# Group 0 of a convolution and mixture kernel: the filter's last product in blocks of 16 frequencies, its first block inside step 1

## The chip, the cores and the metric

The kernel runs on one core of a Trainium2 chip. The metric is the time of one execution on the device in microseconds (us): the median of the runs, 891.58 us before the change, with runs from 891.2 to 893.62. The core has engines that run side by side, each its own instructions in order: TensorE (PE in the profile, with its weight loads as PEld), VectorE (DVE), ScalarE (ACT), GpSimd (POOL) and SyncE (SP), whose queue issues nearly all DMAs here. They wait for each other through semaphores. SBUF is the on-chip memory, PSUM the eight banks into which TensorE writes its products.

## The reference

All data are float32. The convolution part, cut to what matters:

```
x, v: (4, 11456, 128)      pos_emb: (11456, 64)      w1: (64, 64)      w2: (64, 128)
h  = relu(pos_emb @ w1) @ w2 * exp(-0.01 * pos)
u  = x * v
y  = irfft(rfft(u, 2S) * rfft(h, 2S))[:S]      # a long convolution along the sequence
x' = x * y
```

A soft mixture of 8 experts follows on x' (logits, two softmaxes, two small products per expert, and the sum back to 45824 tokens). The change does not touch it.

## The kernel before

**Tiling.** The transform of length 111 x 197 is done as matrix products with tables. The real input leaves J = 99 frequencies k of the short transform to be handled. The 128 channels are taken in G = 8 groups of 16; a group is 64 signals (4 batches x 16 channels), handled as 16 units u of four signals in step 1 and step 3.

**The stages.** First the filter: its hidden layer, and then two products, `filter_first` and `filter_second`, which leave for every frequency a block of F, the spectrum still in terms of the 64 hidden features. Its last product with `w2` (`filter_last`) turns F into the spectrum of all 128 channels. Then for each group: step 1 (`p1`: `first` makes eight pairs of products per unit and `first_out` copies them from PSUM to the tile T), step 2 (`p2`, for four frequencies at a time: products of T with the table W into PSUM, a multiplication by the filter's spectrum on VectorE into a tile `m`, L344, and the two sums that put the complex result back into T, L350 and L351, on GpSimd), step 3 (`p3`, products with `tab3`, copied to E by ScalarE), step 4 and the gate. Step 3 of a group runs together with step 1 of the next. At the end comes the mixture.

**Around the change: group 0.** Group 0's step 1 runs alone. In its step 2 the filter's last product is made on the way: before every eight frequencies, two calls of `filter_last` (four frequencies each) make the spectrum, ScalarE copies it into `ring`, which has two places of eight frequencies, and a DMA writes the part of groups 1 to 7 to the DRAM tensor `hs`. Group 0 takes its own part from `ring`. A place of the ring is written again only when the multiplications that read it are done and its DMA has landed. Between the multiplications VectorE also prepares inputs of group 1's step 1 (`p1_sd`: a product L268, two sums L270, two sums L274; below called a fold), after the 2nd, 6th, 10th and 14th `p2`.

**What sets the order.** Nearly all instructions are wrapped in `inorder`, so each engine runs them as the Python program issues them. PSUM comes from two pools of four banks: `psa` (units 2, 3, 6, 7, ... of step 1 in group 0, and all of step 2, one bank per `p2`) and `psb` (units 0, 1, 4, 5, ... of group 0, and `filter_last`, two banks per call). A bank is used again when its copy or multiplication has read it. The tile `m` has three buffers. The inputs of units 0 to 7 of group 0 lie in the memory of `ring` until step 1 has read them.

Of the kernel before, what the change touches and what calls it, by code (L numbers as in the profile page):

```python
# [13 lines left out]
AF = mybir.ActivationFunctionType  # L14
# [7 lines left out]
J = 99  # L22
# [41 lines left out]
def conv_part(ctx, tc, cp, moe, xf, vf, xi, xe, pos, w1, w2, win, t1x, t1h, wt, t3, t4, hs, scr):  # L64
    nc = tc.nc
# [18 lines left out]
    inorder = tc.keep_in_program_order  # L84
# [11 lines left out]
    HK = 8  # L96
# [112 lines left out]
                                 start=True, stop=True, tile_position=(0, FO * h))  # L209
        nc.scalar.activation(F[:, k0 : k0 + n, :], ps[:, :n, :], AF.Copy)  # L210

    def filter_last(k):

        n = min(4, J - k)
        ps = [psb.tile([N1, 4, G, CG], F32, tag="psb", name=f"fl{s}_{k}") for s in range(2)]
        for i in range(n):
            for s in range(2):
                inorder(nc.tensor.matmul(ps[s][:, i].rearrange("p g c -> p (g c)"),  # L218
                                         lhsT=F[FO * s : FO * s + FO, k + i, :],
                                         rhs=w2s[FO * s : FO * s + FO],  # L220
                                         start=True, stop=True, tile_position=(FO * s, 0)))
        for s in range(2):
            dst = ring[:N1, k // HK % 2, :, k % HK : k % HK + n, CG * s : CG * s + CG]
            inorder(nc.scalar.activation(dst, ps[s][:, :n].rearrange("p k g c -> p g k c"), AF.Copy))  # L224
        if k % HK or k + 4 >= J:
            k0 = k // HK * HK
            n = min(HK, J - k0)
            nc.sync.dma_start(out=hs[:, :, k0 : k0 + n, :].rearrange("g p k x -> p g (k x)"),
                              in_=ring[:HP, k0 // HK % 2, 1:, :n].rearrange("p g k x -> p g (k x)"))
# [100 lines left out]
    def p1(g, u, sd, large=False):  # L330
        first_out(g, u, first(g, u, sd, large))
# [144 lines left out]
    for g in range(G + 1):  # L476

        if g == 0:
            for u in range(NU):
                p1(g, u, sds.pop(u))  # L480
                if u in (9, 11):
                    p1_x(1, PRE + 2 + (u - 9) // 2)
        elif g < G:
            if not pso:
                first_ps.close()
                pso.append(conv_ps.enter_context(tc.tile_pool(name="pso", bufs=2, space=bass.MemoryType.PSUM)))
            def third(us, larges):
                for u, large in zip(us, larges):
                    p3(g - 1, u, large)
                    if u + 2 < NU and u + 2 not in sds:  # L490
                        sds[u + 2] = p1_sd(g, u + 2, nc.vector)

            def behind(u):
                w = u + 6
                if w < NU:
                    p1_x(g, w)
                elif w < NU + PRE and g + 1 < G:
                    p1_x(g + 1, w - NU)

            def spectrum(i0, i1):  # L500
                for k in range(11 * i0, 11 * i1, 11):
                    inorder(nc.sync.dma_start(out=Hs[:HP, k : k + 11], in_=hs[g - 1, :, k : k + 11]))

            large = g > 1
            ps = [first(g, u, sds[u], not large) for u in range(2)]
            third(range(2), (large, large))
            for u in range(2):
                first_out(g, u, ps[u])
                behind(u)
            for w in range(PRE + HV, NU):  # L510
                p1_v(g, w)
            third(range(2, 4), (large, large))
            for u in range(2, 4):
                p1(g, u, sds[u], not large)
                behind(u)
            for b in range(1, NU // 4):
                if b > 1:
                    spectrum(4 * b - 8, 5 * b - 6)
                us = range(4 * b, 4 * b + 4)
                third(us, (large, large, not large, not large))  # L520
                for u in us:
                    p1(g, u, sds[u], large == (u % 4 < 2))
                    behind(u)
            if g + 1 < G:
                for w in range(PRE):
                    p1_v(g + 1, w)
        else:
            x0, x1, x2 = [sm.tile([128, PW], F32, tag="m", name=f"xl_{i}", bufs=3) for i in range(3)]
            spare = [x0, x1, x2] + [spare[i % 2] for i in (next(turns), next(turns))] + [x0, x2]
            turns = count()  # L530
            xvs = [p4_load(g - 1, rb) for rb in ORDER[:5]]
            moe.weights()
            conv_ps.close()
            moe.logit_banks()
            pso[0] = ctx.enter_context(tc.tile_pool(name="psl", bufs=3, space=bass.MemoryType.PSUM,
                                                    reuse_waits="tile"))
            for u in range(NU):
                p3(g - 1, u)
            moe.places()
            moe.steps = _moe(moe)  # L540
            next(moe.steps)

        sds = {}
        nxt_g = g + 1 if g + 1 < G else None

        def ahead(step):
            if nxt_g is None:
                return
            if step == 1:
                for u in range(PRE):  # L550
                    sds[u] = p1_sd(nxt_g, u, nc.vector)
            else:
                for u in range(PRE, PRE + 4):
                    p1_x(nxt_g, u)

        if 0 < g:
            ahead(1)
        ks = list(range(0, J, KB)) if g < G else []
        if g == 0:
            sds = next_sds  # L560
            for i, k in enumerate(ks):
                if k % HK == 0:
                    for w in range(k, min(J, k + HK), 4):
                        filter_last(w)
                p2(g, k)
                if i in (1, 5, 9, 13):
                    u = PRE + i // 4
                    sds[u] = p1_sd(1, u, nc.vector)
            continue
        ex = exs[g % 2]  # L570
        inorder(nc.sync.dma_start(out=ex, in_=xe[g - 1]))
        if g < G:
            xvs = {0: p4_load(g - 1, 0), APART: p4_halves(g - 1, APART), 2: p4_load(g - 1, 2)}
            vcs, done = {}, 0
            for what, n in STEPS:
                if what == "p2":
                    for _ in range(n):
                        p2(g, ks[done])
                        done += 1
                elif what != "gate":  # L580
                    pv = p4(g - 1, n, what)
                    if what:
                        vcs[n] = p4_copy(g - 1, n, pv)
                else:
                    if n == APART:
                        p4_gate_apart(n, xvs[n], pvs[n], vcs[n], ex)
                    else:
                        p4_gate(g - 1, n, xvs[n], pvs[n], vcs[n], ex)
                    if g < G - 1 and n == 5:
                        for u in range(PRE, PRE + HV):  # L590
                            p1_v(g + 1, u)
                    p4_out(g - 1, n, xvs[n])
                    if n == 0:
                        ahead(2)
                    if n in NEXT:
                        xvs[NEXT[n]] = p4_load(g - 1, NEXT[n])
                    if n == 2:
                        xvs[6] = p4_halves(g - 1, 6)
            assert done == len(ks)
            p4_rest(g - 1, ex)  # L600
            continue
        def last_gate(t, rb, xv, pv, vc):
            if t < 4:
                p4_gate(g - 1, rb, xv, pv, vc, ex)
            else:
                p4_gate_apart(rb, [xv[:, PW // 2 * w :][:, : PW // 2] for w in range(2)], pv, vc, ex)
            p4_out(g - 1, rb, xv)
            if t == 5:
                p4_rest(g - 1, ex)
            if t == 3:  # L610
                xvs.append(p4_load(g - 1, ORDER[6]))
            moe.ahead(t)
            if t == 1:
                xvs.append(p4_load(g - 1, ORDER[5]))

        for t, rb in enumerate(ORDER):
            p4(g - 1, rb, 0)
            if t == 6:
                next(moe.steps)
                last_gate(*held)  # L620
            pv = p4(g - 1, rb, 1)
            vc = p4_copy(g - 1, rb, pv)
            held = (t, rb, xvs.pop(0), pv, vc)
            if t == 4:
                moe.spot = wide[rb][:, 0, 2 * NJ : 2 * NJ + 8]
            if t >= 5:
                next(moe.steps)
            if t != 5:
                last_gate(*held)
# [659 lines left out]
```

## Time and profile before

| what | value |
|---|---|
| median of 3 runs | 891.58 us (891.2 to 893.62) |
| profiled execution, span (its own time is given as this alone) | 888.8 us |
| TensorE busy | 858.3 us, 97% |
| VectorE busy | 714.9 us, 80% |
| ScalarE busy | 455.9 us, 51% |
| GpSimd busy | 393.3 us, 44% |
| mean granted TensorE clock | 0.991 |

Busy time of TensorE is that of pipelined instructions whose ends are modelled. Times in the rows are counted from the span's start. In a row of the timeline several like instructions that follow each other stand as one, with their number; what is in square brackets is the time that the engine stood idle before, and who ended it; "issue" there is a wait that the profile can't name. A float32 product of the program appears as two products in the trace.

### The profile page before, as it was taken

The page shows a single profiled execution, that of the slowest core. Times are in us where ns is not written, and L with a number is a line of the kernel's source. Part 1 is how long each engine was busy: PE and PEld are TensorE (multiplying, and loading weights), DVE is VectorE, ACT ScalarE, POOL GpSimd, SP SyncE. Part 2 cuts the span into 40 slices and gives each one's busy share as a digit, 9 for nine tenths or more (in the row PEclk, how much of TensorE's full clock was granted, in tenths as well). Part 3 has the DMA queues.
Part 4 walks back from the last instruction along what each step waited for, and adds up shares of the span by engine and source line. Part 5 has one row for each costly group of instructions (what it writes and reads, how often), then busy time and mean ns, then how long its engine had stood idle before and what let it go on. Part 6 is the DMA issues. An engine that isn't in the chain of part 4 may idle for free. (4 is left out here: it accounts for less than half of the span.)

```text
span 888.8 us, 37282 instructions
## 1 busy us (share of the span) xinstructions
PE 858.3 (97%) x16192; PEld 792.5 (89%) x16192; DVE 714.9 (80%) x1239; ACT 455.9 (51%) x971; POOL 393.3 (44%) x538
## 2 busy tenths in 40 slices
PE   9999999999999999999999999999999999999991
PEld 9998989999999999999999999999999997666540
DVE  5967976898899889988988998899779148886791
ACT  5775558315811751473167128414821637887761
POOL 5003860492088029405910960393079013785750
PEclk9999999999999999999999999999999999999996
DMA  9963685548647755775386476557715979993698
GB/s 329 396 193 117 205 249 148 157 147 269 203 125 210 234 165 141 227 235 167 110 282 201 123 224 207 167 167 238 224 57 166 264 182 374 412 369 121 278 417 364
DMA packets 94386, 197.01 MB, mean 222 GB/s; under 512 B 14330, under 2 KB 55708, under 8 KB 90383
## 3 DMA queue, kind: packets, MB, share of 16 engines
q1 hardware_dynamic: 94046, 194.50, 66.8%
q8 instruction: 127, 2.08, 0.9%
q14 instruction: 37, 0.30, 0.1%
q10 hardware_dynamic: 144, 0.07, 0.0%
q0 software_dynamic: 32, 0.07, 0.0%
HBM read 137.73 MB, written 56.86 MB: 219 GB/s over the span
## 5 line engine op out<-in xcount | busy, mean ns | idle before, releaser
L350 POOL TENSOR_TENSOR T<-m 111x256 f32<-111x256 f32 (+1 forms) x199 | 150.8, 758 | 344.5 <-DVE m L344 344.5
L344 DVE TENSOR_TENSOR m<-p,T 111x1024 f32<-111x1024 f32 (+1 forms) x175 | 200.4, 1206 | 14.4 <-PE p L340 7.0
L360 PE MATMUL p<-tab,T 111*99 111x112 f32 x2048 | 205.4, 260 | 1.5 <-POOL T L351 0.3
L360 PEld LDWEIGHTS p<-tab,T 111*99 111x99 f32 x2048 | 198.8, 170 | 6.5 <-issue 1.6
L340 PE MATMUL p<-T,W 128*64 128x128 f32 (+1 forms) x3168 | 196.7, 276 | 0.4 <-issue 0.3
L420 ACT ACTIVATE vc<-p 128x416 f32<-128x416 f32 x112 | 51.9, 516 | 266.2 <-PE p L411 226.6
L340 PEld LDWEIGHTS p<-T,W 128*64 128x64 f32 (+1 forms) x3168 | 181.8, 127 | 2.7 <-issue 0.9
L411 PE MATMUL p<-tab,E 99*64 99x104 f32 x3584 | 174.1, 252 | 1.1 <-DVE E L373 0.6
L411 PEld LDWEIGHTS p<-tab,E 99*64 99x64 f32 x3584 | 166.4, 136 | 3.1 <-ACT vc L420 0.8
L375 ACT ACTIVATE E<-p 99x448 f32<-99x448 f32 x254 | 132.2, 577 | 63.7 <-PE p L360 57.5
L351 POOL TENSOR_TENSOR T<-m 111x256 f32<-111x256 f32 (+1 forms) x199 | 147.4, 740 | 0.0
L186 ACT ACTIVATE T<-p 128x396 f32<-128x396 f32 x240 | 100.4, 539 | 11.5 <-PE p L174 11.4
L174 PE MATMUL p<-tab1x,x 53*64 53x99 f32 x3648 | 86.7, 246 | 0.2 <-ACT E L224 0.2
L174 PEld LDWEIGHTS p<-tab1x,x 53*64 53x64 f32 x3648 | 79.8, 132 | 4.4 <-ACT E L224 0.4
L436 DVE TENSOR_TENSOR p<-p,vc 128x832 f32<-128x832 f32 x46 | 47.3, 1028 | 10.3 <-ACT vc L420 10.3
L268 DVE TENSOR_TENSOR x<-x,T 128x448 f32<-128x448 f32 x51 | 31.6, 619 | 22.2 <-PE p L174 11.2
L274 DVE TENSOR_TENSOR x<-T 128x224 f32<-128x224 f32 x102 | 39.2, 426 | 1.8
L270 DVE TENSOR_TENSOR T<-x 128x224 f32<-128x224 f32 x102 | 39.2, 425 | 1.7
L224 ACT ACTIVATE E<-fl 111x512 f32<-111x512 f32 (+1 forms) x50 | 26.9, 629 | 21.3 <-PE fl L218 21.3
L444 DVE TENSOR_TENSOR E<-p,E 128x824 f32<-128x824 f32 x36 | 36.6, 1017 | 1.2
L713 ACT ACTIVATE xreg<-pt 128x512 f32<-128x512 f32 (+1 forms) x68 | 35.0, 612 | 0.8 <-PE pt L707 0.7
L344 DVE TENSOR_TENSOR m<-p,E 111x1024 f32<-111x1024 f32 (+1 forms) x25 | 28.7, 1202 | 5.1 <-PE p L340 4.9
(156 smaller groups left out, 972.8 us busy)
## 6 DMA issues: line engine op xcount, KB each, us to landing
x<-in_xf_dram SPq DMA_DIRECT2D x114, 256.0 KB, 4.2
out_dram<-xreg SPq DMA_DIRECT2D x16, 1024.0 KB, 10.5
E<-in_xi_dram SPq DMA_DIRECT2D x37, 412.0 KB, 4.0
T<-in_vf_dram SPq DMA_DIRECT2D x65, 224.0 KB, 5.0
scr<-E SPq DMA_DIRECT2D x67, 206.0 KB, 3.7
T<-hs SPq DMA_DIRECT2D x63, 154.0 KB, 4.5
hs<-E SPq DMA_DIRECT2D x12, 784.0 KB, 4.6
mv<-in_vf_dram SPq DMA_DIRECT2D x42, 224.0 KB, 5.2
```

Of the source, the lines that this page charges most:

```text
L174: inorder(nc.tensor.matmul(ps[h][RP * d : RP * d + RP, i, s, :], lhsT=sd[js, i, s, d, :], rhs=tab1x[js, J * (s + d) : J * (s + d + 1)], st ...
L186: inorder(nc.scalar.activation(dst, src, AF.Copy))
L270: inorder(eng.tensor_tensor(out=vt[:, :, m : m + 2], in0=xr[:, :, 0:2], in1=xr[:, :, 2:4], op=op))
L340: inorder(nc.tensor.matmul(ps[ns, i].rearrange("p b c -> p (b c)"), lhsT=W[:, k0 + i, ns], rhs=Tf[:, :, k0 + i, :], start=True, stop=True, ...
L344: inorder(nc.vector.tensor_mul(m[:, :n].rearrange("p k s e c i -> p k s (e c i)").rearrange("p k s (b c) -> p k s b c", c=CG), ps[:, :n].u ...
L350: inorder(eng.tensor_tensor(out=Ty[:, 0], in0=m[:, :n, 0, 0], in1=m[:, :n, 1, 1], op=ALU.subtract))
L351: inorder(eng.tensor_tensor(out=Ty[:, 1], in0=m[:, :n, 1, 0], in1=m[:, :n, 0, 1], op=ALU.add))
L360: inorder(nc.tensor.matmul(pk[:, i, 2 * s : 2 * s + 2, :].rearrange("p q r -> p (q r)"), lhsT=T[0:N1, s, 2 * k + i, u // 2, :, u % 2], rhs ...
L375: inorder(nc.scalar.activation(dst, src, AF.Copy))
L411: inorder(nc.tensor.matmul(pv[RP * h : RP * h + RP, 2 * k + i, w, :], lhsT=E[:J, r, 2 - 2 * w + s, :], rhs=tab4[:, s, o : o + NJ], start=( ...
L420: inorder(nc.scalar.activation(vc[:, w], pv[:, :, 0, :], AF.Copy, scale=2.0 * w - 1.0))
L436: inorder(nc.vector.tensor_tensor(out=pw, in0=pw[:, 1:2].to_broadcast([128, 2, 4, NJ]), in1=vc, op=ALU.add))
```

## The change

The function `filter_run` makes the last product for up to 16 frequencies in a row (2 x HK), in four calls of `filter_last`. The run of frequencies 0 to 15 stands after unit 7 of group 0's step 1; the others, from 16 on, before every 16 frequencies of step 2. In the third call of each run the copy of the second half (`s` = 1) goes to VectorE in place of ScalarE. Group 1's folds come after the 4th, 8th, 12th and 16th `p2`. What is computed stays the same.

```
     def filter_run(k0):
         for k in range(k0, min(J, k0 + 2 * HK), 4):
             filter_last(k, k == k0 + HK)

@@ filter_last(k, shared)
         for s in range(2):
             dst = ring[:N1, k // HK % 2, :, k % HK : k % HK + n, CG * s : CG * s + CG]
-            inorder(nc.scalar.activation(dst, ps[s][:, :n].rearrange("p k g c -> p g k c"), AF.Copy))
+            src = ps[s][:, :n].rearrange("p k g c -> p g k c")
+            if s and shared:
+                inorder(nc.vector.tensor_copy(out=dst, in_=src))
+            else:
+                inorder(nc.scalar.activation(dst, src, AF.Copy))
@@ step 1 of group 0
             for u in range(NU):
                 p1(g, u, sds.pop(u))
+                if u == NU // 2 - 1:
+                    filter_run(0)
@@ step 2 of group 0
             for i, k in enumerate(ks):
-                if k % HK == 0:
-                    for w in range(k, min(J, k + HK), 4):
-                        filter_last(w)
+                if k and k % (2 * HK) == 0:
+                    filter_run(k)
                 p2(g, k)
-                if i in (1, 5, 9, 13):
+                if i in (3, 7, 11, 15):
                     u = PRE + i // 4
                     sds[u] = p1_sd(1, u, nc.vector)
```

On ScalarE around the second half of step 1, before. In a name such as p_0_8_0 stand the group, the unit and the half; fl_4 is a bank of the filter's last product from frequency 4 on.

```order
L186 ACTIVATE T<-p_0_7_0_986 128x2x198
L186 ACTIVATE T<-p_0_8_0_1006 128x2x198
L186 ACTIVATE T<-p_0_9_0_1026 128x2x198
L186 ACTIVATE T<-p_0_10_0_1048 128x2x198
L186 ACTIVATE T<-p_0_11_0_1068 128x2x198
L186 ACTIVATE T<-p_0_12_0_1090 128x2x198
L186 ACTIVATE T<-p_0_13_0_1110 128x2x198
L186 ACTIVATE T<-p_0_14_0_1130 128x2x198
L186 ACTIVATE T<-p_0_15_0_1150 128x2x198
L224 ACTIVATE E<-fl_0_1170 111x8x4x16
L224 ACTIVATE E<-fl_0_1171 111x8x4x16
```

The same place on ScalarE in the changed program:

```order
L186 ACTIVATE T<-p_0_7_0_986 128x2x198
L232 ACTIVATE E<-fl_0_1006 111x8x4x16
L232 ACTIVATE E<-fl_0_1007 111x8x4x16
L232 ACTIVATE E<-fl_4_1018 111x8x4x16
L232 ACTIVATE E<-fl_4_1019 111x8x4x16
L232 ACTIVATE E<-fl_8_1031 111x8x4x16
L232 ACTIVATE E<-fl_12_1043 111x8x4x16
L232 ACTIVATE E<-fl_12_1044 111x8x4x16
L186 ACTIVATE T<-p_0_8_0_1056 128x2x198
L186 ACTIVATE T<-p_0_9_0_1076 128x2x198
```

Seven copies of the filter stand between the units 7 and 8; the eighth, the second half of fl_8, is VectorE's.

On VectorE at the beginning of step 2, before. m_8 is the multiplication for frequencies 8 to 11, the instructions on x_2 are the fold of unit 2 of group 1.

```order
L188 COPY T<-p_0_15_1_1151 128x2x198
L344 TENSOR_TENSOR m_0_1204<-p_0_0_1195,E 111x1024
L344 TENSOR_TENSOR m_4_1217<-p_0_4_1208,E 111x1024
L268 TENSOR_TENSOR x_2_577<-x_2_577,T 128x8x56
L270 TENSOR_TENSOR T<-x_2_577 128x2x112 x2
L274 TENSOR_TENSOR x_2_577<-T 128x4x56 x2
L344 TENSOR_TENSOR m_8_1260<-p_0_8_1251,E 111x1024
L344 TENSOR_TENSOR m_12_1273<-p_0_12_1264,E 111x1024
L344 TENSOR_TENSOR m_16_1311<-p_0_16_1302,E 111x1024
L344 TENSOR_TENSOR m_20_1324<-p_0_20_1315,E 111x1024
L268 TENSOR_TENSOR x_3_579<-x_3_579,T 128x8x56
```

The same place on VectorE in the changed program:

```order
L188 COPY T<-p_0_15_1_1201 128x2x198
L352 TENSOR_TENSOR m_0_1229<-p_0_0_1220,E 111x1024
L352 TENSOR_TENSOR m_4_1242<-p_0_4_1233,E 111x1024
L352 TENSOR_TENSOR m_8_1255<-p_0_8_1246,E 111x1024
L352 TENSOR_TENSOR m_12_1268<-p_0_12_1259,E 111x1024
L276 TENSOR_TENSOR x_2_577<-x_2_577,T 128x8x56
L278 TENSOR_TENSOR T<-x_2_577 128x2x112 x2
L282 TENSOR_TENSOR x_2_577<-T 128x4x56 x2
L230 COPY E<-fl_24_1303 111x8x4x16
L352 TENSOR_TENSOR m_16_1336<-p_0_16_1327,E 111x1024
L352 TENSOR_TENSOR m_20_1349<-p_0_20_1340,E 111x1024
```

The fold stands two multiplications later, and behind it VectorE's copy of the filter (fl_24), ahead of the next multiplication.

## Rows read from the trace of the kernel before

**Rows 1.** The page: busy us (share of the span), instructions; a queue's packets, MB.

```profile
PE 858.3 (97%) x16192; PEld 792.5 (89%) x16192; DVE 714.9 (80%) x1239; ACT 455.9 (51%) x971; POOL 393.3 (44%) x538
...
q8 instruction: 127, 2.08, 0.9%
```

**Rows 2.** Stretches: length, busy of PE, PEld, DVE, ACT, POOL, clock, DMA, GB/s.

```profile
77.40:126.10 48.70, 48.29 (x826) 44.07 (x824) 44.50 (x47) 26.10 (x49) 39.47 (x48) 1.00 0.69 204
126.10:888.00 761.90, 736.44 (x14036) 676.75 (x14036) 616.95 (x1066) 379.34 (x819) 342.62 (x474) 0.99 0.67 218
```

**Rows 3.** Timeline of VectorE, step 2: start, length, line, operation, number [idle before].

```profile
78.63 2.36 DVE L344 TENSOR_TENSOR m<-p,E 111x1024 f32<-111x1024 f32 x2 [2.46 <-PE p L340]
...
84.80 4.60 DVE L344 TENSOR_TENSOR m<-p,E 111x1024 f32<-111x1024 f32 x4
...
89.97 1.65 DVE L270 TENSOR_TENSOR T<-x 128x224 f32<-128x224 f32 x2
...
93.23 4.60 DVE L344 TENSOR_TENSOR m<-p,E 111x1024 f32<-111x1024 f32 x4
...
110.07 6.87 DVE L344 TENSOR_TENSOR m<-p,E 111x1024 f32<-111x1024 f32 x6
117.81 2.36 DVE L344 TENSOR_TENSOR m<-p,E 111x1024 f32<-111x1024 f32 x2 [0.88 <-PE p L340]
121.72 2.36 DVE L344 TENSOR_TENSOR m<-p,E 111x1024 f32<-111x1024 f32 x2 [1.55 <-PE p L340]
124.30 0.96 DVE L344 TENSOR_TENSOR m<-p,E 111x768 f32<-111x768 f32 x1 [0.23 <-ACT E L224]
...
125.97 0.35 DVE L351 TENSOR_TENSOR T<-m 111x192 f32<-111x192 f32 x1
```

**Rows 4.** Timeline of all engines, the first blocks of eight frequencies.

```profile
75.45 2.00 PE L218 MATMUL fl<-E 64*111 64x128 f32 x32
...
76.61 2.16 ACT L224 ACTIVATE E<-fl 111x512 f32<-111x512 f32 x4 [0.57 <-PE fl L218]
...
77.39 2.04 PE L340 MATMUL p<-T,W 128*64 128x128 f32 x32
...
79.35 1.80 PEld L218 LDWEIGHTS fl<-E 64*111 64x111 f32 x32 [0.18 <-issue]
...
80.51 2.17 ACT L224 ACTIVATE E<-fl 111x512 f32<-111x512 f32 x4 [1.74 <-PE fl L218]
```

**Rows 5.** Timeline of all engines, the beginning of step 3.

```profile
126.15 3.41 PE L360 MATMUL p<-tab,T 111*99 111x112 f32 x32 [0.29 <-POOL T L351]
...
129.18 1.89 ACT L375 ACTIVATE E<-p 99x448 f32<-99x448 f32 x4 [4.99 <-DMA hs<-E]
...
129.78 3.31 PE L360 MATMUL p<-tab,T 111*99 111x112 f32 x32 [0.22 <-ACT E L375]
...
130.43 0.69 DVE L270 TENSOR_TENSOR T<-x 128x224 f32<-128x224 f32 x2
```

**Rows 6.** Timeline of VectorE, the last units of step 1.

```profile
74.92 1.26 DVE L188 COPY T<-p 128x396 f32<-128x396 f32 x2 [1.60 <-PE p L174]
```

**Rows 7.** Groups by line from 20 to 140 us: count, busy us, mean ns, idle before.

```profile
L188 DVE COPY T<-p 128x396 f32<-128x396 f32 x16 | 9.1, 571 | 9.8 <-PE p L174 8.5
```

**Rows 8.** Timeline of TensorE's products, step 1.

```profile
66.23 1.50 PE L174 MATMUL p<-tab1x,E 53*64 53x99 f32 x58 [0.29 <-issue]
67.50 0.24 PE L174 MATMUL p<-tab1x,x 53*64 53x99 f32 x1
...
69.68 2.97 PE L174 MATMUL p<-tab1x,mv 53*64 53x99 f32 x127 [0.47 <-issue]
73.92 1.60 PE L174 MATMUL p<-tab1x,mv 53*64 53x99 f32 x63 [1.27 <-issue]
```

**Rows 9.** The page's groups: count, busy us, mean ns of one, idle before.

```profile
L224 ACT ACTIVATE E<-fl 111x512 f32<-111x512 f32 (+1 forms) x50 | 26.9, 629 | 21.3 <-PE fl L218 21.3
```

**Rows 10.** Timeline of GpSimd in step 2.

```profile
111.36 0.74 POOL L350 TENSOR_TENSOR T<-m 111x256 f32<-111x256 f32 x1 [1.46 <-DVE m L344]
112.05 0.74 POOL L351 TENSOR_TENSOR T<-m 111x256 f32<-111x256 f32 x1
```

More of the change, by code (lines that the diff above doesn't have):

```diff
@@ L210, in filter_second, with filter_run, filter_last @@
         nc.scalar.activation(F[:, k0 : k0 + n, :], ps[:, :n, :], AF.Copy)
-    def filter_last(k):
+    def filter_run(k0):
+        for k in range(k0, min(J, k0 + 2 * HK), 4):
+            filter_last(k, k == k0 + HK)
+    def filter_last(k, shared):
         n = min(4, J - k)
```

## The prediction, written before the changed kernel ran

> **What bounds the kernel now.** I read the page's busy shares first. TensorE is busy 97% of the span, VectorE 80% [rows 1], and everything that the change touches lies in group 0, so the share of the whole says little and the stage has to be read by itself. The table by stretches does that: from the first product of group 0's step 2 (77.4) to the first of the next step (126.1) TensorE is busy 48.3 of 48.7 us, but VectorE also 44.5 and GpSimd 39.5; after it TensorE is busy 736 of 762 us [rows 2]. So a shift at 126 us should pass on to the end nearly whole, and inside the stage two engines are close to the bound. VectorE's timeline shows how close: from 84.80 to 116.94 its instructions follow each other without a wait, in cycles of 8.43 us for 16 frequencies (84.80 to 93.23: four multiplications L344 in 4.60, then the five instructions of a fold `p1_sd`). It is behind TensorE there. Only after the last fold does it catch up and wait (0.88 and 1.55 us) [rows 3]. TensorE's own 16 frequencies take 7.8 us (75.45 to 79.35 for eight) [rows 4]. In step 2, then, TensorE never waits because VectorE's arrears, 0.6 us a cycle, just fit into four product banks. Step 3 begins at 126.15, when VectorE's L351 (125.97 plus 0.35) and GpSimd are through; its third unit begins at 129.78, when the copy that waited for the last `hs` write is done [rows 3, 5].
>
> Step 1 of group 0 is the other place. A unit takes 0.69 us there (two VectorE copies end 1.26 us after the first began, a copy is 0.57 long) [rows 6, 7]. But TensorE pauses "for issue" at 66.23, 69.68 and 73.92, each time after 128 products, 3.45 and 4.24 us apart, where 128 products need 2.76 [rows 8]. Instruction fetches are a queue of their own [rows 1], so I read these pauses as TensorE running ahead of them.
>
> **The change part by part.** The sum is made against the profiled execution, span 888.8 us. The median of the runs shown is 891.58; I take the 2.8 us between them as work outside the span that does not change.
>
> *The first 16 frequencies amid step 1.* Removed at the end of step 1: the block of eight at 75.45, 1.94 us [rows 4]. Added after unit 7: four calls of `filter_last`, begun where unit 8 began, at 67.50 [rows 8]. Each call takes two of four banks of `psb`, so the third and fourth call need the copies of the first and second. A block's first copy starts 1.16 us after its first product (75.45 to 76.61), four copies take 2.16 and one is 0.63 long, so they start 0.51 apart [rows 4, 9]. The third call's second bank is free 1.16 + 0.51 + 0.63 = 2.30 us after the run's start, the fourth's 1.16 + 3 x 0.51 + 0.63 = 3.32; that call is half of a block's 1.80 [rows 4], and the run ends at 4.2. It would be 3.6 without the two waits. Unit 9 needs the bank of the fourth call's second copy: 4.2 + 0.29 + 0.51 + 0.63 = 5.6 (0.29 is 1.16 less the first call's 0.87 to 0.9). Units 9 to 15 take 7 x 0.69, so the last ends at 67.50 + 5.6 + 4.8 = 77.9. Now a cover is gone: step 2's first product waits for unit 15's copies, which ended 0.88 us after its last product (unit 15 began at 73.92 + 0.69, its copy ended at 74.92 + 1.26) [rows 6, 8], and were hidden by the block at 75.45. That makes 78.8 against 77.39, with the pauses at 69.68 and 73.92 (0.7 and 1.5 us beyond 2.76) already taken as gone, since the run gives the fetch 4 us. They come back in part: the next 128 products begin at 71.7, unit 12 is due 3.5 us later, step 2 another 3.6 us on, and the fetch has needed 3.45 to 4.24: 0 to 0.8 and 0 to 0.6 us. I take 0.7 for both. Term A: **+2.1 us** (1.4 to 2.8).
>
> The Trainium skill, "Runtime: NRT & Kernel Launch", Instruction fetch mechanics, says that instructions come in blocks of 256 and that the fetch is mostly hidden. The trace agrees on the block (128 products, each with its weight load) and not on the hiding. Were the pauses not fetches, they would stay; that is the fourth rival.
>
> *Step 2 in blocks of 16.* Per 16 frequencies one change from the filter's products to the main ones and one back go away. Eight frequencies take 3.90 us (75.45 to 79.35), of which the products themselves need about 3.6 (1.80 a block by the weight loads), so 0.3 a pair [rows 4]. Against it stand the waits of the second half of a run for banks, 0.6 as above. TensorE alone would gain 1.8 (two more of the calls that left step 2, at 0.9) + 6 x 0.3 and lose 5 x 0.6: about -0.5 us.
>
> *VectorE's copies.* One in each full run, five of them in step 2. The trace has no such copy; a copy of 396 columns takes 0.57 [rows 7], a multiplication of 1024 columns 1.2 and 1.13 to the next (6.87 for six) [rows 3], so 512 columns take between 0.5 and 0.7; by the slope between the two, 0.69 long and 0.61 to the next. It stands behind a fold and ahead of the multiplications of its own frequencies, so everything queued behind it moves by 0.61: a cycle becomes 9.04. The folds move from i = 1, 5, 9, 13 to 3, 7, 11, 15, behind four multiplications as before, so GpSimd has the same arrears beside them and I keep 8.43. (Alone, a pair of a fold's instructions takes 0.69 instead of 1.65 [rows 3, 5].)
>
> VectorE from step 2's first product T: 1.24 until the first multiplication (77.39 to 78.63) [rows 3, 4], four cycles 36.2, so T + 37.4. The run of frequency 80 needs the bank that the copy of 72 then leaves: 4.2 of run, 0.1 of change, 1.24 to the first multiplication of 80: T + 42.95, where VectorE is free at 37.4 + 4 x 1.13 + 0.61 = 42.55. Four more, 4.53, and the tail from 124.30 to 126.32, 2.02 [rows 3]: T + 49.5. GpSimd works off the last eight at 2 x 0.69 [rows 10], from T + 38.6 to T + 49.7. Step 3 starts at about T + 49.6; before it was 126.15 - 77.39 = 48.76. Term B: **+0.85** (0, if the folds shorten and TensorE bounds, to 1.7, with copies of 0.7 and waits at each turn of banks).
>
> *The rest.* ScalarE loses six copies, but it stood idle 1.74 us ahead of a block [rows 4]; nothing. The loads of x_4 and x_5 go behind two `hs` writes on the SP queue, more than 20 us ahead of their folds; nothing. The last `hs` write moves with the run of 96 and lands no later relative to step 3 than now.
>
> Sum: 2.1 + 0.85 = +2.95 us, 891.58 + 3 = **894.6 us**.
>
> **The rivals.** (1) TensorE bounds step 2, because the folds fall where GpSimd is idle: 16 half-fold instructions at 0.35 instead of 0.83 give VectorE 7.7 us back. For it: VectorE waited at the end of the stage. Against: GpSimd is 39.5 of 48.7 us busy. Then B is -0.5 and the time 891.58 + 2.1 - 0.5 = 893.2. (2) Faster: the filter's first run lies wholly in TensorE's pauses. It decides whether ScalarE empties banks as fast as TensorE fills them, so that a run takes 3.6 and not 4.2, in step 1 and five times in step 2, and unit 9 does not wait; with no pause returning, A is 2.1 - 0.6 - 0.6 - 0.7 = 0.2 and B -0.5 - 5 x 0.6 = -3.5: 888.3. Against: two copies need 1.02 us to start, a call 0.9, and VectorE would have to shed the same 3 us. (3) The delay arises but is absorbed behind 129.78, where TensorE has 25 us of idle time to the end [rows 2]: 891.6. Against: its third unit now waits only 0.22 for a landing [rows 5]. (4) The pauses belong to units 6, 10 and 14, not to fetches, and stay: 2.2 - 0.7 = 1.5 more, 896.1. Against: the even 128 products.
>
> **How the numbers follow.** Forecast 0.57, (1) 0.19, (2) 0.08, (3) 0.09, (4) 0.07. The forecast's own range, from its terms' bounds, is 893.0 to 896.1. The whole range, 891.8 to 896.6, leaves out (2) and ends of the others. A measurement of this kernel tells about 0.3% from no change, 2.7 us: 888.9 to 894.25. Of the forecast three quarters lie above (the hand-overs between the engines are not in the sum, and each adds), of (4) nearly all: 0.43 + 0.07 = 0.50 slower; of (1) and (3) nearly all lie inside, with a quarter of the forecast: 0.42; faster 0.08.
>
> **What would show it.** In step 1 of the new profile: the main products of step 2 starting at about 79.5, VectorE's first multiplication 1.2 later, TensorE waiting for ScalarE twice in the run after unit 7, no long issue pause at units 10 and 14. In step 2: VectorE without waits in cycles of 9.0 us until the last fold, TensorE waiting for VectorE's copies before the runs of 64 and 80, step 3 at 129. The forecast is wrong if VectorE waits for TensorE between folds (then 1), if the runs have no inner wait (2), or if step 3 starts late and the end does not (3).

## The result, and the profile after

The changed kernel takes **897.16 us** (median of 5 runs, 893.2 to 900.24) beside 891.25 for the kernel before in the same session: ratio 1.0059, 95% interval 1.0036 to 1.0082, or +5.3 us (3.2 to 7.3). It is slower. The forecast was +2.95 us, so its direction held and its sum was 2.3 us short; the median lies 0.6 us above the upper end of the whole range (896.6).

The profiled execution was the shortest of the five, 893.2 us with a span of 891.2. Its page hardly differs from [rows 1]; the stretches that answer to [rows 2] follow, with the columns given there:

```profile
78.90:128.70 49.80, 48.74 (x792) 44.36 (x793) 47.59 (x52) 20.38 (x37) 39.38 (x48) 1.00 0.57 170
128.70:890.20 761.50, 736.28 (x14036) 676.73 (x14036) 616.78 (x1066) 378.93 (x819) 342.65 (x475) 0.99 0.67 218
```

Behind step 3's first product nothing has changed: 762.5 us to the span's end (891.2 - 128.7), before 762.6. The loss lies ahead of 128.7. TensorE's products in step 1, which answer to [rows 8], and VectorE's timeline of step 2, which answers to [rows 3]:

```profile
60.80 5.73 PE L174 MATMUL p<-tab1x,E 53*64 53x99 f32 x256
66.46 4.49 PE L222 MATMUL fl<-E 64*111 64x128 f32 x64
70.88 1.92 PE L174 MATMUL p<-tab1x,x 53*64 53x99 f32 x62
...
78.89 3.88 PE L348 MATMUL p<-T,W 128*64 128x128 f32 x64 [1.86 <-issue]
...
128.70 0.41 PE L368 MATMUL p<-tab,T 111*99 111x112 f32 x2 [0.49 <-POOL T L358]
```

```profile
72.92 4.70 DVE L188 COPY T<-p 128x396 f32<-128x396 f32 x7 [0.46 <-PE p L174]
80.13 4.62 DVE L352 TENSOR_TENSOR m<-p,E 111x1024 f32<-111x1024 f32 x4 [2.50 <-PE p L348]
...
88.56 0.68 DVE L230 COPY E<-fl 111x512 f32<-111x512 f32 x1
89.16 4.60 DVE L352 TENSOR_TENSOR m<-p,E 111x1024 f32<-111x1024 f32 x4
...
98.18 4.60 DVE L352 TENSOR_TENSOR m<-p,E 111x1024 f32<-111x1024 f32 x4
...
121.08 0.69 DVE L230 COPY E<-fl 111x512 f32<-111x512 f32 x1 [0.25 <-PE fl L222]
122.19 5.48 DVE L352 TENSOR_TENSOR m<-p,E 111x1024 f32<-111x1024 f32 x5 [0.42 <-PE p L348]
```

In the kernel before, step 1 began here:

```profile
61.44 4.49 PE L174 MATMUL p<-tab1x,E 53*64 53x99 f32 x194
```

Step 2 starts 18.09 us behind step 1 (78.89 - 60.80; before 77.39 - 61.44 = 15.95), step 3 another 49.81 later (128.70 - 78.89; before 48.76). The three pauses of [rows 8] have become one, ahead of step 2: unit 15's last copy ended at 77.62 (72.92 + 4.70) and the first main product came 1.27 us after. VectorE runs without a wait from 80.13 to 120.8, in cycles of 9.02 to 9.03 us (80.13, 89.16, 98.18). This execution, the fastest, fits the forecast (+2.14 for a term of 2.1, +1.05 for 0.85). In the first term that is in part luck: the pause beyond the copies was 0.57 us longer than the 0.7 that I took, but the pause at 66.23 [rows 8], which I had left in, was gone, and the run with its copies took 0.14 less. The median doesn't fit, so something that varies from execution to execution is missing.

### The profile page after: what moved, and what is told of

Read it like the earlier page. It is cut to its first block, busy times and chain, and to the rows that moved or that the text cites. A ratio compares the mean times of both kernels' runs of the same rounds, so it can differ in the third digit from the quotient of the medians.

```text
span 891.2 us, 37283 instructions
## 1 busy us (share of the span) xinstructions
PE 860.2 (97%) x16192; PEld 794.3 (89%) x16192; DVE 718.5 (81%) x1245; ACT 452.6 (51%) x965; POOL 393.2 (44%) x538
## 5 line engine op out<-in xcount | busy, mean ns | idle before, releaser
L232 ACT ACTIVATE E<-fl 111x512 f32<-111x512 f32 (+1 forms) x44 | 24.3, 624 | 29.7 <-PE fl L222 29.1
L1130 PE MATMUL pw<-cs,so 32*128 32x512 f32 (+2 forms) x192 | 31.8, 610 | 0.7 <-DVE xreg L1137 0.7
```

The source lines that it names most:

```text
L1130: inorder(nc.tensor.matmul(po[:, :na].rearrange("p k t -> p (k t)"), lhsT=so[NSLOT * a : NSLOT * a + NSLOT], rhs=ct[NSLOT * a : NSLOT * a ...
```

## Experiments

Each kernel was compared with runs of the kernel before on its own chip, whose medians were 891.2 to 891.8 us. Packet times below were read from the trace's records of the instruction queue.

**The changed kernel again.** Nothing edited.

> The changed kernel as it is, once more. The sum of the prediction gives +3 us over the kernel before, and the one profiled execution agrees (step 3 begins 2.9 us later, counted from the start of step 1). The five timed runs lie 2 to 9 us higher, with granted clocks of 0.988 to 0.991. Theory 1 (only the sum): a new profile shows the same step 1 and 2 and the median is 894 to 895. Theory 2 (something more, in most executions: the clock falls after the pause between the steps, or the first loads land later): the median is again near 897, and a profile of such an execution has a stretch at clock 0.5 before 130 us, or step 1 begins later than 61.4.

897.0 us; 1.0064 (1.0041 to 1.0088). Its profiled execution, 897.74 us, is a typical one. VectorE and TensorE around the start of step 2, and the stretches behind it:

```profile
73.53 4.71 DVE L188 COPY T<-p 128x396 f32<-128x396 f32 x7 [0.47 <-PE p L174]
83.15 1.23 DVE L352 TENSOR_TENSOR m<-p,E 111x1024 f32<-111x1024 f32 x1 [4.91 <-PE p L348]
...
92.68 4.60 DVE L352 TENSOR_TENSOR m<-p,E 111x1024 f32<-111x1024 f32 x4
```

```profile
61.15 5.99 PE L174 MATMUL p<-tab1x,E 53*64 53x99 f32 x256
...
81.06 5.43 PE L348 MATMUL p<-T,W 128*64 128x128 f32 x64 [3.43 <-issue]
86.41 4.49 PE L222 MATMUL fl<-E 64*111 64x128 f32 x64
...
132.21 0.41 PE L368 MATMUL p<-tab,T 111*99 111x112 f32 x2 [0.44 <-POOL T L358]
```

```profile
81.00:84.40 3.40, 3.34 (x32) 3.34 (x34) 1.23 (x1) 0.00 (x0) 0.00 (x0) 0.51 0.02 5
84.40:88.00 3.60, 3.60 (x64) 3.42 (x62) 3.22 (x3) 0.43 (x1) 3.34 (x5) 0.99 0.00 0
```

The copies were through at 78.24, and the pause lasted 2.82 us beyond them. Then TensorE's granted clock was 0.5 (1.2 GHz) for 3.4 us, and the block of 64 took 5.43 us where it takes 3.88 at 2.4 GHz. From step 1 to step 2 went 19.91 us, from step 2 to step 3 51.15. VectorE's second four multiplications begin 11.62 us behind step 2's start (92.68 - 81.06), where the first profile has 10.27 (89.16 - 78.89): of the 1.55 us of the slower block 1.35 reach the stage. Less these it takes 49.80, term B as in the first profile. The spans of the two executions are 4.1 us apart (895.3 and 891.2), and 3.2 of them lie here: 1.82 ahead of step 2, of which the pause is 1.55 (2.82 less 1.27), and 1.34 in it, by the clock.

**Parts taken back.** `no_step1` puts the first run of 16 back to the head of step 2, `no_vector` gives all copies to ScalarE, `no_folds` takes the four folds out of step 2.

```
no_step1: -                if u == NU // 2 - 1:
          -                    filter_run(0)
          ...
          -                if k and k % (2 * HK) == 0:
          +                if k % (2 * HK) == 0:
no_vector: `if s and shared` made never true
no_folds: -                if i in (3, 7, 11, 15):   (and the fold under it)
```

> The changed kernel with its first run of 16 frequencies at the head of step 2 instead of amid step 1; all else stays. If the run amid step 1 is what costs (the bank waits of unit 9, the bared copies of unit 15), the time falls by about 2 us against the changed kernel. If it only moves work that has to be done somewhere, and the run of 16 waits for its banks wherever it stands, the time stays within 0.5 us of the changed kernel (+3 us over before), TensorE waits for ScalarE at the head of step 2, and the pauses for issue in step 1 are back at units 10 and 14. If the extra time of most executions comes from the pause of TensorE before step 2, it is gone here.

> The changed kernel with all copies of the filter on ScalarE. If VectorE bounds step 2, a cycle of 16 frequencies falls from 9.0 to 8.4 us, step 3 begins about 1 us earlier than in the changed kernel and the time is 1 us lower (+2 us over before). If the banks bound, the fourth call of a run waits for one copy of ScalarE more and the time stays or rises by 0.5 us.

> The changed kernel without the four folds in step 2; they are made in step 3 of group 1, as the other folds of that group. If VectorE bounds step 2, its 16 us of folds no longer count, VectorE waits for TensorE in each block, and the time falls to where TensorE and the banks bound: about 1.2 us below the changed kernel (+2 us over before). If VectorE did not bound, nothing changes (+3). If the cost lies in VectorE alone, the time falls to that of the kernel before or below.

`no_step1`: 894.59 us, 1.0036 (1.0022 to 1.0051), some 2.4 us below the changed kernel (the intervals overlap) although it has the same blocks and copies. TensorE pauses in step 1 again (0.48, 0.98), but not ahead of step 2:

```profile
62.30 6.04 PE L174 MATMUL p<-tab1x,E 53*64 53x99 f32 x253
...
74.24 1.60 PE L174 MATMUL p<-tab1x,mv 53*64 53x99 f32 x63 [0.98 <-issue]
75.78 4.49 PE L222 MATMUL fl<-E 64*111 64x128 f32 x64
80.19 3.88 PE L348 MATMUL p<-T,W 128*64 128x128 f32 x64
```

Its step 2 starts 17.89 us behind step 1 (80.19 - 62.30), hardly earlier than the 18.09 of the changed kernel's fastest execution. By these profiles a first run of 16 in one piece delays step 2 by some 2 us, amid step 1 as at the head of step 2, and what is gone here is the long pause that other executions of the changed kernel have.

`no_vector`: 896.25 us, 1.0052 (1.0034 to 1.007). Step 3 came 49.00 us behind step 2 (128.63 - 79.63), 0.81 less than with the copies (49.81), and VectorE's cycle is 8.43 again (80.88 to 89.31). So the copies make most of term B (0.81 of the 1.05 measured). In the total the interval can't tell it. This profile is of its fastest execution (894.33): step 2 waits for copies and not for issue.

```profile
80.88 4.62 DVE L352 TENSOR_TENSOR m<-p,E 111x1024 f32<-111x1024 f32 x4 [1.99 <-PE p L348]
...
89.31 4.60 DVE L352 TENSOR_TENSOR m<-p,E 111x1024 f32<-111x1024 f32 x4
```

```profile
79.63 3.88 PE L348 MATMUL p<-T,W 128*64 128x128 f32 x64 [1.39 <-DVE T L188]
...
128.63 0.41 PE L368 MATMUL p<-tab,T 111*99 111x112 f32 x2 [0.54 <-POOL T L358]
```

`no_folds`: 896.98 us, 1.0061 (1.0039 to 1.0082): no gain that the intervals show. VectorE now waits for TensorE in every cycle, here twice in one cycle:

```profile
107.50 0.69 DVE L230 COPY E<-fl 111x512 f32<-111x512 f32 x1 [1.43 <-PE fl L222]
109.69 4.62 DVE L352 TENSOR_TENSOR m<-p,E 111x1024 f32<-111x1024 f32 x4 [1.50 <-PE p L348]
```

and a cycle still takes 8.2 us (the next block's multiplications begin at 117.92): TensorE's own bound in blocks of 16. Its pause ahead of step 2 was 3.51 us, again with 3.4 us at a clock of 0.5 behind it.

**A cover over the pause, and the pause moved.** `cover` parts the first run: calls 0 and 4 behind unit 7, 8 and 12 behind unit 15. `shift` puts 44 more products into TensorE's stream, long before step 1.

```
cover: -                if u == NU // 2 - 1:
       -                    filter_run(0)
       +                if u in (NU // 2 - 1, NU - 1):
       +                    for w in (0, 4) if u < NU - 1 else (HK, HK + 4):
       +                        filter_last(w, w == HK)
shift: ...
       -    idle_products(4)
       +    small_products(48)
```

> The first sixteen frequencies' calls are parted: 0 and 4 amid step 1 as in the changed kernel, 8 and 12 behind unit 15, between step 1 and step 2. Theory (bare fetch and clock): the changed kernel loses beyond the forecast because TensorE's pause ahead of step 2, 1.3 to 3.5 us, lies bare, and because a pause of 3.4 us is followed by 3.4 us at a granted clock of 0.5; two calls (2.2 us) put over that place leave a pause under 1.3 us there, no stretch at 0.5, step 2 17.0 to 17.9 us behind step 1, and 893.5 to 894.8 us in all. Rival (the blocks of sixteen cost more in step 2 than forecast, whatever stands ahead of it): 896 to 898 us, as the changed kernel.

> The changed kernel with its four idle products ahead of the filter's first product replaced by 48 small ones (16 columns by 16), so that every later TensorE instruction stands 44 products, or 88 records, later in the stream; nothing else moves. The pauses of step 1 stood 128 records apart, the last at the first main product of step 2. Theory (a pause belongs to a place in the instruction stream): none ahead of step 2; the pause falls 40 records behind its start, where VectorE still has three mixtures to do. Step 2 starts within 0.6 us of unit 15's last copies, no stretch at 0.5 follows, and the time is 893.0 to 895.5 us with up to 1.4 us lost to the small products ahead of step 1. Rival (the pause belongs to the change from step 1 to step 2, with its waits for sixteen units' copies): 1.3 to 3.5 us of pause stay ahead of step 2, and the time is 896.5 to 898.5 us.

`cover`: 893.67 us, 1.0019 (1.0009 to 1.003), an interval that ends below the changed kernel's (1.0041 to 1.0088). The pause shrinks to 0.38, step 2 starts 16.87 us behind step 1 (I had said 17.0 to 17.9), and the clock stays at 2.4 GHz there:

```profile
75.56 2.00 PE L222 MATMUL fl<-E 64*111 64x128 f32 x32
77.94 3.90 PE L348 MATMUL p<-T,W 128*64 128x128 f32 x64 [0.38 <-issue]
```

Step 2 itself takes the changed kernel's 49.8 us, so the runs of 16 in step 2 do not carry the excess. (One of the first run's two `hs` writes moved behind step 1 with its calls, so `cover` also has less DMA traffic in step 1; see below.) `shift`: 895.04 us, 1.0034 (1.0021 to 1.0048).

```profile
74.88 2.47 PE L179 MATMUL p<-tab1x,mv 53*64 53x99 f32 x102
77.96 2.12 PE L179 MATMUL p<-tab1x,mv 53*64 53x99 f32 x87 [0.61 <-issue]
80.88 3.87 PE L353 MATMUL p<-T,W 128*64 128x128 f32 x64 [0.81 <-DVE T L193]
```

The pause stands 87 recorded records ahead of step 2 (one may be missing), where the 88 added ones put it, and step 2 waits only for copies. The rest of what I expected failed: 40 records into step 2, one period of 128 later, there is no pause, and what came is the 0.61 inside unit 13. So a pause belongs to a place in the instruction stream.

**Other parts done alone.** `step1_only` is the kernel before with the run of 16 behind unit 7; `blocks16_only` is the kernel before with blocks of 16.

```
step1_only: +                if u == NU // 2 - 1:
            +                    for w in range(0, 2 * HK, 4):
            +                        filter_last(w)
            ...
            -                if k % HK == 0:
            +                if k >= 2 * HK and k % HK == 0:
blocks16_only: -                if k % HK == 0:
               -                    for w in range(k, min(J, k + HK), 4):
               +                if k % (2 * HK) == 0:
               +                    for w in range(k, min(J, k + 2 * HK), 4):
```

> The kernel before with the first sixteen frequencies amid step 1 and nothing else: blocks of eight from frequency 16 on, all copies on ScalarE, folds where they were. Theory (bare fetch and clock): the last pause of step 1 stands ahead of step 2 as in the changed kernel; d from the start of step 1 to that of step 2 is 17.5 to 20 us (15.95 before), and the time is 893.5 to 896 us. Rival (only the forecast's two terms, 2.1 us for this part, some of which comes back as step 2 has one block of eight fewer): 892.5 to 893.5 us, with a pause under 0.6 us.

> The kernel before with blocks of sixteen in step 2, the first at its head, all copies on ScalarE, folds where they were. Theory (bare fetch and clock): no pause ahead of step 2, since the run of sixteen lies over it; what stays is the wait of VectorE for each run of sixteen, 2.0 to 2.8 us in all: 893.3 to 894.5 us. Rival (blocks of sixteen carry the whole loss): 896 to 897.5 us.

`step1_only`: 894.74 us, 1.0038 (1.0024 to 1.0051), with the pause (its copies ended at 78.88) and the slow block:

```profile
81.77 5.45 PE L340 MATMUL p<-T,W 128*64 128x128 f32 x64 [3.50 <-issue]
87.16 2.00 PE L218 MATMUL fl<-E 64*111 64x128 f32 x32
```

`blocks16_only`: 894.67 us, 1.0035 (1.0022 to 1.0047), without a pause ahead of step 2. The median lies 0.2 above the theory's range, and 1.3 below the rival's. Alone the two parts lose 3.4 and 3.1 us, 6.5 in sum; the changed kernel loses 5.3 (3.2 to 7.3), so these runs can't say whether the losses add.

**What holds the fetch up.** In the profiles a pause ended 2.2 to 2.9 us after a 16 KB packet of the instruction queue had begun. These packets come one after another; ahead of step 2 they stood so (the last column is the share of the 16 DMA engines' time that the other queues took between the two packets):

| kernel | packet before | packet | apart | first product behind it | other queues |
|---|---|---|---|---|---|
| before (unit 14) | 67.33 | 71.42 | 4.09 | 73.92 | 42% |
| no_step1 | 71.76 | 75.39 | 3.63 | 80.19, no pause | 8% |
| cover | 70.73 | 75.50 | 4.77 | 77.94 | 81% |
| no_vector | 72.68 | 77.35 | 4.67 | 79.63, waits for copies | 99% |
| after | 70.78 | 76.65 | 5.87 | 78.89 | 99% |
| again | 71.38 | 78.72 | 7.34 | 81.06 | 93% |
| no_folds | 72.42 | 79.71 | 7.29 | 82.16 | 94% |
| step1_only | 72.73 | 79.47 | 6.74 | 81.77 | 93% |

In the last five, the two `hs` writes that the run of 16 issues, 784 KB each, moved into step 1 with it, beside the loads of x; in `cover` one of them did. The DMA queues of `again` between its two packets, and then around the second (packets, MB, share of 16 engines' time):

```profile
q1 hardware_dynamic: 1805, 2.03, 94.3%
...
q1 hardware_dynamic: 17, 0.03, 7.5%
q8 instruction: 1, 0.02, 6.1%
```

The engines were 94% busy with other traffic, and the instruction packet came when that ended. It is not always so. Between the two packets of `after`, in the microsecond around the second, and between the two of `no_vector`:

```profile
q1 hardware_dynamic: 1598, 1.69, 100.5%
...
q1 hardware_dynamic: 168, 0.27, 76.9%
...
q1 hardware_dynamic: 1295, 1.33, 99.7%
```

There the packet came amid the traffic, in `no_vector` after 4.67 us. So a packet beside this traffic can be late by some 3 us, and need not be. The distance alone is no measure of a wait either: in `shift` the packet ahead of its pause of 0.61 us came 6.38 us after the one before (69.25 and 75.63), but TensorE was busy with the run until 73.11. The test is the changed kernel with the first two writes issued by ScalarE behind unit 15's copies:

```
-        if k % HK or k + 4 >= J:
+        if k > 2 * HK and (k % HK or k + 4 >= J):
...
+            for k0 in (0, HK):
+                inorder(nc.scalar.dma_start(out=hs[:, :, k0 : k0 + HK, :]..., in_=ring[:HP, k0 // HK % 2, 1:, :]...))
```

> The changed kernel with the first two hs writes (frequencies 0 to 15) issued by ScalarE behind unit 15's copies instead of by SP amid step 1; every instruction of TensorE stands where it stood, and the writes carry the same bytes. In the runs so far the 16 KB packet ahead of step 2's first products began 5.9 to 7.3 us after the packet before it wherever the hs writes ran beside it, and 3.4 to 4.1 us after it where they did not, and step 2 began 2.2 to 2.5 us behind that packet. Theory (the hs writes and the x loads, in the same DMA engines, hold up TensorE's instruction fetch): that packet comes 3.4 to 4.5 us after the one before, step 2 starts within 0.6 us of unit 15's last copies, 16.6 to 17.5 us behind step 1 (18.1 to 19.9 in the changed kernel), no stretch at a granted clock of 0.5 follows, and the time is 892.3 to 894.3 us. Rival (the fetch is late for a reason of TensorE's own, such as the bank waits of the run or the place in the stream): the packet comes 5.9 to 7.3 us after the one before, a pause of 1.3 to 3.5 us stays ahead of step 2, and the time is 895.5 to 898 us.

894.31 us, 1.0034 (1.0021 to 1.0047). The queues between the two packets (71.97 and 76.30, 4.33 us apart), and the starts of the steps:

```profile
q1 hardware_dynamic: 246, 0.47, 37.8%
```

```profile
61.37 1.87 PE L174 MATMUL p<-tab1x,E 53*64 53x99 f32 x76
...
79.20 3.88 PE L348 MATMUL p<-T,W 128*64 128x128 f32 x64 [1.06 <-DVE T L188]
...
129.03 0.41 PE L368 MATMUL p<-tab,T 111*99 111x112 f32 x2 [0.48 <-POOL T L358]
```

Step 2 waits for copies, which ended at 78.75, 0.45 us before, and no slow stretch follows. It starts 17.83 us behind step 1; I had said 16.6 to 17.5, with too little for the copies. What stays is +3.0 us (1.9 to 4.2). Packet and pause are the theory's and not the rival's, and the time lies at the upper end of the theory's range. But what I wrote ahead of this run, that the packet came 5.9 to 7.3 us after the one before wherever the writes ran beside it, leaves out `cover` (4.77) and `no_vector` (4.67), which was as quick with both writes beside it. One profile does not decide it then, and the intervals of `late_write` and `again` overlap (to 1.0047, from 1.0041). That the writes make the long pause is the likely cause, not a proven one.

**Versions to keep.** All are the kernel before with single calls drawn into step 1: `parted8` has 0 and 4 behind unit 7, 8 and 12 behind unit 15; `four_calls` has one call behind each of units 8, 10, 12 and 15 (both in blocks of eight from 16 on); `two_calls` has call 0 behind unit 11 and 4 behind 15.

```
two_calls: +                for w in {11: (0,), 15: (4,)}.get(u, ()):
           +                    filter_last(w)
           ...
           -                if k % HK == 0:
           +                if k >= HK and k % HK == 0:
```

> The kernel before with the first sixteen frequencies ahead of step 2, calls 0 and 4 amid step 1 (behind unit 7), 8 and 12 behind unit 15, then blocks of eight from frequency 16 on; all copies on ScalarE, folds where they were. Theory (bare pause and runs of sixteen each carry a part): no pause over 0.6 us and no stretch at a granted clock of 0.5 ahead of step 2, step 2 16.5 to 17.2 us behind step 1 (15.95 before), step 3 46.7 to 48.0 us behind step 2 (48.76 before), and 890.3 to 892.5 us in all: no loss that can be measured. Rival (any filter call amid step 1 costs its bank waits, whatever covers the pause): 893 to 895 us.

> The kernel before with its first block of eight drawn into step 1, call 0 behind unit 11 and call 4 behind unit 15, blocks of eight from frequency 8 on, nothing else moved. One call at a time finds free banks, so no wait for banks is expected. Theory: step 2 starts as it did or up to 0.5 us earlier against step 1, and 890.8 to 892.2 us: same as before within 0.1 per cent. Rival (every change from one product shape to the other inside step 1 costs more than its 0.3 us): 892.5 to 893.5 us.

> The kernel before with the first sixteen frequencies drawn into step 1 as four single calls, behind units 8, 10, 12 and 15, then blocks of eight from frequency 16 on, nothing else moved. Theory (a call alone finds its banks free; three more shape changes at some 0.3 us each; one block of eight fewer in step 2): step 2 17 to 18 us behind step 1, step 3 46.7 to 47.6 us behind step 2, 890.0 to 892.0 us in all: if any version is faster than the kernel before, this one, by up to 1.5 us. Rival (a pause of over 1.3 us comes bare somewhere in step 1 again): 893 to 896 us.

`parted8`: 891.39 us, 1.0006 (0.9997 to 1.0014). `four_calls`: 891.06 us, 1.0003 (0.9993 to 1.0013); it was to be the fastest, and is not. In both, step 2 started earlier than expected, 16.0 and 16.1 us behind step 1, and step 3 came 48.2 us behind step 2, later than expected: the block that step 2 lost was TensorE's, and VectorE's cycles of 8.4 us stayed. `two_calls`: 890.18 us, **0.9989 (0.9978 to 0.9999)**, 1.0 us faster than before, 0.6 below its range, and the fastest kernel here, if barely: it is one of three versions, and its interval ends at 0.9999. Its calls find their banks free, take 1.13 us each, and the second covers unit 15's copies:

```profile
69.84 1.60 PE L174 MATMUL p<-tab1x,mv 53*64 53x99 f32 x62 [0.48 <-issue]
71.37 1.13 PE L218 MATMUL fl<-E 64*111 64x128 f32 x16
72.43 3.58 PE L174 MATMUL p<-tab1x,mv 53*64 53x99 f32 x128
75.94 1.13 PE L218 MATMUL fl<-E 64*111 64x128 f32 x16
77.00 2.04 PE L340 MATMUL p<-T,W 128*64 128x128 f32 x32
```

The pause that stood at 73.92 [rows 8] is gone, where call 0 gave the fetch 1 us, and the first `hs` write is issued at 78.27, behind the packet that step 2 needs (74.84). Step 2 starts 15.17 us behind step 1 instead of 15.95.

## Why the prediction was right in sign and short in size

- **Term A, the run amid step 1: right.** The run was to end 4.2 us after its start and ended after 4.42 (66.46 to 70.88); unit 15's copies were to end 11.3 us after its start (78.8 - 67.50) and did after 11.16 (77.62). The two pauses inside step 1 went, as said, and the cover over unit 15's copies was lost, as said.
- **Term A, the pauses that come back: this step failed.** "They come back in part: ... 0 to 0.8 and 0 to 0.6 us. I take 0.7 for both", from a fetch that "has needed 3.45 to 4.24". Those figures are from a step 1 without the writes. The run drags its own `hs` writes into it, and beside them a packet came 5.9 to 7.3 us after the one before in four profiles of five. The pause beyond the copies was then 1.27, 2.82, 2.90 and 2.89 us (after, again, no_folds, step1_only) instead of 0.7; in the fifth, `no_vector`, it was 0.74. That a bare pause of this length is what the sum lacks, `again` and `cover` show; that the writes lengthen it is likely, as said above. I had seen those writes on the SP queue, and asked only whether the loads behind them would be late, not what else uses the DMA engines.
- **The clock: not in the sum.** The three profiles with a pause of 3.43 to 3.51 us have a granted clock of 0.5 for 3.4 us from within 0.8 us of its end, 1.55 us on a block of 64. Those with 1.86 or less have none there. That a long pause brings the fall is read from these rows; no run lengthened a pause by itself.
- **Without the long pause the forecast's sum stands**: `late_write` has everything of the change but that, and measures +3.0 (1.9 to 4.2) for +2.95. In its profile step 2 starts 1.88 us later against step 1 than before (for 2.1), and step 3 1.07 later against step 2 (129.03 - 79.20 = 49.83; for 0.85). That execution, the slowest of its seven, lost another 2.2 us behind step 3's start, which no run explains.
- **Term B: right.** Copy 0.68 long and 0.60 to the next (0.69 and 0.61 forecast), cycles of 9.03 (9.04), folds unshortened, step 3 at T + 49.81 (49.6); 49.80 in `again` without the slow block. One reading in it was wrong, without harm: VectorE's L351 ended at 126.32, behind step 3's first product at 126.15, which waited for GpSimd's [rows 3, 5].
- **Rivals.** (1) TensorE as the bound: no, VectorE did not wait until 121; and `no_folds` shows TensorE's own bound, 8.2 us a cycle in blocks of 16, where the prediction's figures make 8.1 (7.8 for blocks of eight, less one change of 0.3, and waits of 0.6): VectorE's 9.03 lie above it. (2) no: the run's bank waits came. (3) no: 762.5 us behind step 3's start, as before. (4) named 896.1, nearest to the result, by a wrong mechanism: the pauses do not belong to units, `shift` moved one along the stream.

The Trainium skill, "Runtime: NRT & Kernel Launch", Instruction fetch mechanics, has the sequencer fetch the next block over a DMA queue of its own while the current one runs. The trace agrees that the queue is separate (q8). It does not show the fetch hidden: with the engines 93 to 99% busy with other queues the packet ahead of step 2 came 4.67 to 7.34 us after the one before, and in four of these five profiles TensorE stood still for it.

Open: why the packet needed 4.67 us in one execution and 7.34 in another beside the same writes, and how much of the 2.3 us between the changed kernel and `late_write` is pause and how much clock.

## What to carry to other kernels

Work that is moved takes its transfers with it: ask what its DMA will run beside, instruction fetches included, and try big writes behind the packet that the next stage needs (here 897.0 to 894.3 us, with intervals that still overlap). A pause that costs nothing under a cover costs its whole length, and perhaps the clock, once the cover is moved. Fill such pauses in single calls whose banks are free rather than in one long run: here two single calls gained 1.0 us (0.1 to 2.0), and four gained nothing that could be measured.

## What the runs showed of the hardware beyond that

In step 1 of the kernels without the moved writes (before, no_step1, blocks16_only, two_calls) TensorE's instruction packets follow each other 3.4 to 4.1 us apart; 128 products there take 2.76 us, and TensorE runs ahead of them.

The clock can fall near the end of the program too. In `blocks16_only` (as in `no_step1` and `shift`) it was 0.5 for 3.4 us from 861, shortly behind a wait of 0.72 us of TensorE; the changed kernel's profile has the same wait (0.71) and no fall. Both kernels' stretches, first `blocks16_only`:

```profile
861.00:864.40 3.40, 3.40 (x18) 1.52 (x16) 2.44 (x6) 1.82 (x4) 2.45 (x3) 0.50 1.01 419
```

```profile
861.00:864.40 3.40, 3.40 (x25) 1.58 (x24) 2.93 (x6) 2.49 (x6) 0.00 (x0) 1.00 1.00 417
```

What that costs these profiles don't tell: from step 3's start to the end went 764.9 us in `blocks16_only`, 763.9 in `no_step1` and 762.5 in `shift`, but also 764.9 in `late_write`, without this fall. So a single profile's span says less than the stage's own start times. Nor does the mean clock of an execution: it counts the time behind TensorE's last product as well, 874.0 to 888.7 in the kernel before, where the granted clock is 0.5 and TensorE is busy for 0.00 us.
